# Products of the h and o layers of three batches issued as twins on the two column halves of TensorE

## The chip, the cores and the metric

The kernel runs on one core of a Trainium2 chip. The metric is the time of one execution on the device in microseconds. A profiled execution shows five engines: TensorE (PE, with its weight loads as PEld), VectorE (DVE), ScalarE (ACT), GpSimd (POOL) and SyncE (SP, which issues most DMAs).

## The reference

```python
# attention: 4 batches, 8 heads, 768 positions, 64 wide; proj is 64 x 6
q_bits = (q @ proj > 0); k_bits = (k @ proj > 0)
q_bucket = sum(q_bits * 2**arange(6)); k_bucket = sum(k_bits * 2**arange(6))
scores = where(q_bucket[:, None] == k_bucket[None, :], q @ k.T / 8, -1e9)
x = softmax(scores) @ v                      # heads side by side: (4, 768, 512)
# mixing and channel layer: w_ch1 is 512 x 2048, w_ch2 is 2048 x 512
u = x + real(fft(fft(x, axis=1), axis=2))
un = (u - mean(u)) / sqrt(var(u) + 1e-6)     # over the 512 channels
out = u + maximum(un @ w_ch1, 0) @ w_ch2
```

All inputs and the output are fp32.

## The kernel before

**Attention.** Two heads are handled together; the index n runs over the 16 pairs of heads (4 per batch), and c over six tiles of 128 key positions. For each n and c, `weigh` computes the scores transposed: two products per half of the queries, one per head. Their contraction has 64 rows, so head 0 stands on the upper 64 rows of the array and head 1 on the lower 64 (`sc`, L885). ACT takes the exponential (L889). `values` (L906) multiplies by the values. Each of its products has 64 stationary columns: head 0 stands on the array's left column half and head 1 on its right, and the two share a PSUM bank, on different partitions (`oo`). These are the value products that the title's twins resemble. For one pair, six such steps accumulate.

**Buckets.** `prepare(n+1)` makes the bucket masks for the next pair while the current one runs. `bits` (L817) is four products with 32 columns each and leaves, in the 128 rows of `bt`, the bits of queries and keys of both position halves, 32 rows each. For the pairs 0 to 4 (`LITE`) the bits go straight into the scores as an additional product (L878). For pairs 5 to 15, two more groups follow. `qb` (L831) spreads a number per query over all 128 partitions: for each head h, one product per position half g, with the 32 rows of that half and a table `pw` of powers of two. `kb` (L841) has six tiny products, 128 key positions by two heads each. Then one DVE instruction per head and c compares them and masks the exponentials (L895).

**Mixing.** `mix(b)` does the two Fourier transforms of batch b as products with tables (`cs` L1078, `A` and `B` L1107).

**The channel layer.** `mlp7(b)` computes both layers by a scheme with seven products in place of eight for a 2 by 2 split. The first layer is `h` (`product` at L1371, matmul at L1382): for each of 8 pairs of 128-row blocks there are seven products p1 to p7, each of two steps (k) of 128 by 128 stationary values against 384 moving columns. `h_p` is their PSUM bank. The second layer is `o` (`product` in `outer7`, matmul at L1262): two halves of three tile pairs with seven products of four steps, each 128 by 128 against 256 columns. Each of these results is evacuated from PSUM by ACT or DVE, and combined by DVE. `across` (L1133) transposes rows of x between them.

**Order of the work.** A batch's mixing and channel layer is laid between the attention steps of the next batch: the loop at L1503 takes one step of `attention(b)` and then so many steps of `other`, the generator of `mix(b-1)`, that both end together. So batches 0 to 2 have their h and o products among scores and value products, and batch 3 has them alone, at the end. A scheduler sets each engine's order after that, except in the block under `manual_schedule` (L1473), where the order is as written. `behind()` (L858) puts a product with a raised priority after the last one that was noted in `last[0]`:

```python
with tc.issue_after(last[0].ins), tc.high_priority(offset=AHEAD):
    yield
```

It is used for scores, values, `qb` and `kb`. The h and o products carry no such note. PSUM banks come in three pools of two: `ps_sc` (scores, qb, kb; two banks each), `ps_o` (oo) and `ps_1` (all else, h and o among it), handed out in turn.

Of the kernel before, what the change touches and what calls it, by code (L numbers as in the profile page):

```python
# [11 lines left out]
F32 = mybir.dt.float32  # L12
BF16 = mybir.dt.bfloat16
# [7 lines left out]
P = 128  # L21
B, H, S, D = 4, 8, 768, 64
# [27 lines left out]
def _consts():  # L50


    s = np.arange(HALF)
    freq = np.concatenate([2 * np.arange(NK), 2 * np.arange(NK) + 1])
    ang = 2.0 * np.pi * (np.outer(s, freq) % S) / S
    seq = np.stack([np.cos(ang), np.sin(ang)])
    seq = seq.reshape(2, NT // 2, P, 2 * NK).transpose(2, 0, 1, 3)


    d = np.arange(DM // 2)  # L60
    ang = 2.0 * np.pi * (np.outer(d, np.arange(DM)) % DM) / DM
    sin = -np.sin(ang)
    sin[0] = 1.0 - 2.0 * (np.arange(DM) % 2)
    chan = np.concatenate([np.cos(ang), sin]).reshape(NDC, P, DM).transpose(1, 0, 2)

    off = np.zeros((P, 2))
    for h in range(2):
        off[h * D : h * D + NBITS] = 0.5  # L70
        off[h * D + NBITS] = (NBITS / 4.0, -1.0)


    pw = np.zeros((P, 2, P))
    for r in range(P):
        h, bit = divmod(r % 32, NBITS)
        if h < 2:
            pw[r, h] = 2.0**bit


    d = np.arange(DM // 2)
    fr = np.concatenate([np.arange(DM // 2 + 1), np.arange(1, DM // 2)])
    ang = 2.0 * np.pi * (np.outer(d, fr) % DM) / DM
    ch = np.where(np.arange(DM) <= DM // 2, np.cos(ang), np.sin(ang))
    ch = ch.reshape(2, P, DM // 2, 2).transpose(1, 0, 3, 2)

    s = np.concatenate([np.arange(2, HALF // 2, 2), np.arange(1, HALF // 2, 2)])  # L90
    rows = np.concatenate([s, [0, HALF // 2], s])
    kind = np.repeat([0, 1, 2, 3], [len(s), 1, 1, len(s)])
    sq = np.zeros((2, 2, P, HALF + 1))
    for par in range(2):
        cols = slice(par * NK, HALF + 1 if par else NK)
        ang = 2.0 * np.pi * (np.outer(rows, freq[: HALF + 1][cols]) % S) / S
        for k in range(2):
            own = kind == (0 if par == k else 3)
            own |= (kind == 1) & (k == 0) | (kind == 2) & (k == par)
            w = np.where(own[:, None], np.sin(ang) if k else np.cos(ang), 0.0)  # L100
            w = w.reshape(NT // 2, P, -1)
            sq[0, k, :, cols] = w[0 if par == k else 2]
            sq[1, k, :, cols] = w[1]
    sq = sq.transpose(2, 0, 1, 3)
    return {
        "pw": np.ascontiguousarray(pw, dtype=np.float32),
        "ch": np.ascontiguousarray(ch, dtype=np.float32),
        "sq": np.ascontiguousarray(sq, dtype=np.float32),
        "seq": np.ascontiguousarray(seq, dtype=np.float32),
        "chan": np.ascontiguousarray(chan, dtype=np.float32),  # L110

        "off4": np.ascontiguousarray(np.tile(off[:32], (4, 1)), dtype=np.float32),
        "off": np.ascontiguousarray(off, dtype=np.float32),
    }
# [367 lines left out]
def _main(  # L482
# [109 lines left out]
    nc.gpsimd.memset(pj, 0.0)  # L592
    for h in range(2):
        nc.sync.dma_start(pj[h * D : (h + 1) * D, h * NBITS : (h + 1) * NBITS], proj)
    pw = const.tile([P, 2, P], BF16, tag="pw", name="pw")
    ones = const.tile([P, 32], F32, tag="ones", name="ones")
    nc.gpsimd.memset(ones, 1.0)
    mhalf = const.tile([P, 1], F32, tag="mhalf", name="mhalf")
# [150 lines left out]
    def prepare(n):  # L749
# [76 lines left out]
        for h in range(2):  # L826
            ps = ps_sc.tile([P, 2, 512], F32, tag="sc", name=f"qb{n}_{h}")
            for g in range(2):
                rows = slice(32 * g, 32 * g + 32)
                with behind() if g + h else nullcontext():  # L830
                    last[0] = nc.tensor.matmul(  # L831
                        ps[:, g, 0:HALF], pw[rows, h, :], bt[rows, :],
                        start=True, stop=True,
                    )
            evac(qb[:, h, :].rearrange("p (g s) -> p g s", g=2), ps[:, :, 0:HALF])
        ps = ps_sc.tile([P, 2, 512], F32, tag="sc", name=f"kb{n}")
        for c in range(NT):
            g, i = divmod(c, NT // 2)
            rows = slice(64 + 32 * g, 96 + 32 * g)
            with behind() if c else nullcontext():  # L840
                last[0] = nc.tensor.matmul(  # L841
                    ps[:, g, 2 * i : 2 * i + 2], bt[rows, i * P : (i + 1) * P],
                    pw[rows, :, 0], start=True, stop=True,
                )
        nc.vector.tensor_copy(
            kb.rearrange("p h (g i) -> p g i h", g=2),
            ps[:, :, 0:NT].rearrange("p g (i h) -> p g i h", h=2),
        )
        preps[n] = ts["q"], ts["k"], qb, kb

# [177 lines left out]
    def fold(b, cp):  # L1028
# [6 lines left out]
        for pc in range(2):  # L1035
# [22 lines left out]
            )  # L1058
            yield

    def mix(b):
        x = xs[b]
        yield from fold(b, 1)
        z = zs[b]


        hd = DM // 2
        F = wt([P, 2, 2, 2, DM], F32, "F", f"F{b}", 1)
        nc.gpsimd.memset(F[:, :, 1, :, 0 : hd + 1 : hd], 0.0)
        for par in range(2):  # L1070
            for t in range(NT // 2):
                ps = pt([P, DM], f"cs{b}_{par}_{t}")
                kinds = (0, 1) if t == 1 else (par ^ (t // 2),)
                for pc in range(2):
                    lo = 0 if 0 in kinds else hd // 2 + 1 - pc
                    hi = hd if 1 in kinds else hd // 2 + 1 - pc
                    for cp in range(2):
                        nc.tensor.matmul(  # L1078
                            ps[:, pc + 2 * lo : pc + 2 * hi - 1 : 2],
                            z[:, cp, pc, par, t * P : (t + 1) * P],  # L1080
                            ch[:, cp, pc, lo:hi], start=(cp == 0), stop=(cp == 1),
                        )
# [14 lines left out]
                yield  # L1097

        for j in range(NDC):
            pa, pb = (pt([P, HALF + 1], f"{nm}{b}_{j}") for nm in "AB")
            for par in range(2):
                cols = slice(par * NK, HALF + 1 if par else NK)
                for k, ps in enumerate((pa, pb)):
                    for t in range(2):
                        nc.tensor.matmul(  # L1107
                            ps[:, cols], F[:, par, k, t, j * P : (j + 1) * P],
                            sq[:, t, k, cols], start=(t == 0), stop=(t == 1),
                        )  # L1110

            for ps, op in (pa, ALU.add), (pb, ALU.subtract):
                for i in range(2):
                    u = x[:, j, i * HALF : (i + 1) * HALF].rearrange("p (r n) -> p r n", r=2)
                    if i == 0:
                        f = ps[:, 0 : 2 * NK - 1]
                        f = bass.AP(f.tensor, f.offset, [f.ap[0], [NK, 2], [1, HW]])
                    else:
                        f = ps[:, HW : HALF + 1]
                        f = bass.AP(f.tensor, f.offset, [f.ap[0], [HW, 2], [-1, HW]])  # L1120
                    nc.vector.tensor_tensor(
                        u, u, f, op=op if (j < 2) ^ i else ALU.add
                    )
            yield

        yield from mlp7(b)
# [110 lines left out]
    def outer7(b, half, hall, ut, rs, s1s):  # L1237
# [14 lines left out]
        for j in range(GT):  # L1252
# [4 lines left out]
            def product(a, i, ps=None):  # L1257
# [1 line left out]
                if start:  # L1259
                    ps = pt([P, HD], f"o{b}_{half}_{j}_{i}")  # L1260
                for r in range(HF // 2):
                    nc.tensor.matmul(  # L1262
                        ps, a[:, r], right7[i][:, r], start=start and r == 0,
                        stop=r == HF // 2 - 1, skip_group_check=not start,
                    )
                if j == GT - 1 and (b < B - 1 if half else b > 0):
                    nc.sync.dma_start(right7[i], bd[1 - half, i])
# [57 lines left out]
    def mlp7(b):  # L1325
# [45 lines left out]
        def product(i, ps, start=True):  # L1371
# [7 lines left out]
                    c, r = (0 if i == A11 else 2), (f + HF if i == A22 else f)  # L1379
                    left = w1[:, c : c + 2, r * P : (r + 1) * P]  # L1380
            for k in range(2):
                nc.tensor.matmul(  # L1382
                    ps, left[:, k], right[i][:, k],
                    start=start and k == 0, stop=k == 1, skip_group_check=not start,
                )
            done[0] += 1
            fetch()
# [85 lines left out]
    with tc.manual_schedule(engines={ET.PE, ET.DVE, ET.Activation, ET.Pool}):  # L1473
# [5 lines left out]
                next(other, None)  # L1479
        for _ in other:  # L1480
            pass
        pwf = wt([P, 2, P], F32, "ef", "pwf", 1)
        nc.sync.dma_start(pwf, cn["pw"].ap())
        nc.scalar.copy(pw, pwf)
        means = []
# [100 lines left out]
```

## Time and profile before

| what | value |
|---|---|
| median of 3 runs (lowest to highest) | 1102.68 us (1102.34 to 1106.73) |
| span of the profiled execution | 1100.8 us |
| that execution's own time beside its span | not recorded apart; the fastest run shown is 1.5 us and the median 1.9 us above the span |
| mean granted clock of TensorE | 0.995 |
| PE busy | 1054.5 us, 96% |
| PEld busy | 629.4 us, 57% |
| DVE, ACT, POOL busy | 786.5, 500.6, 58.6 us |
| o products on PE (L1262, three groups) | 259.4 + 42.3 + 3.9 us |
| h products on PE (L1382, five groups) | 163.1 + 105.5 + 23.8 + 23.7 + 12.8 us |
| values on PE (L906), scores on PE (L885) | 155.1, 159.8 us |

Busy time is the union of an engine's records. A row of a group reads: line, engine, operation, what it writes and reads, the shape (rows by columns of the array, then the moving operand), the number of records, then busy time and mean duration, then the engine's idle time before it and what ended that. A timeline row reads: start, length, engine, line, operation, shape and how many records were merged in it.

### The profile page before, as it was taken

Reading aid. Unit: us, or ns where it says so; the run is one execution under the profiler, and the core shown is the slowest. Engines: PE = TensorE matmul, PEld = TensorE weight load, DVE = VectorE, ACT = ScalarE, POOL = GpSimd, SP = SyncE. Lnnn points to the kernel's source line nnn. Section 1 sums busy time; section 2 is a strip of 40 time slices with the busy share of each in tenths; the row PEclk is TensorE's granted clock in tenths of the full one; section 3 lists DMA queues with packets and bytes.
Section 4 is the critical chain, followed back from the end, with each engine's and each line's share of the span. In section 5 each row is a group of like instructions: output and inputs, shape, how many; then the busy total and the mean of one; then the engine's idle time right before and its main releaser. Section 6 shows DMA issues by size and latency. Waiting matters only on the chain.

```text
span 1100.8 us, 14127 instructions
## 1 busy us (share of the span) xinstructions
PE 1054.5 (96%) x4933; PEld 629.4 (57%) x4933; DVE 786.5 (71%) x1321; ACT 500.6 (45%) x1055; POOL 58.6 (5%) x132
## 2 busy tenths in 40 slices
PE   7999997999989999999999999999999999999996
PEld 2333354446744675545664576645674569768675
DVE  5798958868699977776767785965856785644353
ACT  6888555653276324454326433355315522340420
POOL 0000000002000020010000011001000002100000
PEclk9999999999999999999999999999999999999998
DMA  8745443441056161322144134213032205122401
GB/s 224 221 90 119 76 123 88 149 147 26 20 139 210 46 204 34 66 61 70 26 157 108 48 73 162 44 39 96 15 121 75 68 24 172 54 82 85 126 20 41
DMA packets 175566, 103.13 MB, mean 94 GB/s; under 512 B 129408, under 2 KB 162816, under 8 KB 175488
## 3 DMA queue, kind: packets, MB, share of 16 engines
q1 hardware_dynamic: 169696, 88.65, 29.9%
q0 software_dynamic: 4224, 13.11, 3.8%
q8 instruction: 41, 0.67, 0.3%
q10 hardware_dynamic: 1568, 0.39, 0.2%
q14 instruction: 37, 0.30, 0.1%
HBM read 81.14 MB, written 20.97 MB: 93 GB/s over the span
## 4 chain that ended last, share of the span: by engine, by line
PE 63%; DVE 11%; ACT 4%; DMA 2%; issue 2%; DVEq 0%; SPq 0%; ACTq 0%
PE o L1262 22%; PE h_p L1382 21%; PE oo L906 7%; PE sc L885 6%; DVE pk L895 3%; PE cs L1078 2%; PE A L1107 2%; DMA zraw<-in_moe_w_ch_dram 2%; PE B L1107 1%; DVE acc L980 1%; ACT rr L940 1%; PE bits L817 1%; DVE w L1274 1%; DVE h L1248 1%; PE un L1133 1%
## 5 line engine op out<-in xcount | busy, mean ns | idle before, releaser
L1262 PE MATMUL o<-w,h 128*128 128x256 f32 x1152 | 259.4, 382 | 1.2 <-ACT tq L1281 0.7
L1262 PEld LDWEIGHTS o<-w,h 128*128 128x128 f32 x1152 | 216.3, 190 | 43.6 <-issue 4.6
L889 ACT ACTIVATE pk<-sc 128x768 f32<-128x768 f32 x192 | 148.5, 809 | 81.6 <-PE sc L885 64.5
L1382 PE MATMUL h_p<-x,w 128*128 128x384 f32 x448 | 163.1, 494 | 3.2 <-ACT h L1404 1.7
L885 PE MATMUL sc<-qt,kt 64*128 64x384 f32 x768 | 159.8, 519 | 5.4 <-ACT pk L889 5.1
L906 PE MATMUL oo<-pk,vn 128*64 128x385 f32 (+1 forms) x768 | 155.1, 499 | 4.0 <-DVE pk L895 3.3
L895 DVE SCALAR_TENSOR_TENSOR pk<-qb,kb,pk 128x768 f32<-128x768 bf16 x132 | 129.0, 1013 | 29.5 <-ACT pk L889 29.4
L1382 PEld LDWEIGHTS h_p<-x,w 128*128 128x128 f32 x448 | 82.0, 190 | 70.6 <-ACT pk L889 5.4
L980 DVE TENSOR_TENSOR acc<-acc,pk 128x1536 f32<-128x1536 f32 (+1 forms) x72 | 105.8, 1483 | 6.1 <-ACT pk L889 5.4
L1382 PE MATMUL h_p<-w 128*128 128x384 f32 x288 | 105.5, 489 | 2.3 <-ACT w L1419 2.3
L906 PEld LDWEIGHTS oo<-pk,vn 128*64 128x64 f32 x768 | 49.1, 136 | 97.8 <-issue 68.7
L885 PEld LDWEIGHTS sc<-qt,kt 64*128 64x128 f32 x768 | 62.9, 185 | 56.1 <-issue 29.6
L1382 PEld LDWEIGHTS h_p<-w 128*128 128x128 f32 x288 | 53.7, 190 | 41.7 <-ACT w L1419 3.5
L1292 ACT COPY tq<-o 128x256 f32<-128x256 f32 x24 | 8.9, 373 | 105.1 <-PE o L1262 105.1
L1274 DVE SCALAR_TENSOR_TENSOR w<-o,rs,w 128x256 f32<-128x256 f32 x56 | 26.8, 479 | 41.6 <-PE o L1262 41.6
L1262 PE MATMUL o<-w 128*128 128x256 f32 x176 | 42.3, 383 | 1.4 <-DVE w L1274 1.3
L1408 DVE TENSOR_TENSOR h<-h 128x384 f32<-128x384 f32 x32 | 17.8, 556 | 32.2 <-ACT h L1407 32.2
L1281 ACT COPY tq<-o 128x256 f32<-128x256 f32 x24 | 8.9, 371 | 69.3 <-PE o L1262 69.2
L1262 PEld LDWEIGHTS o<-w 128*128 128x128 f32 x176 | 32.8, 190 | 8.8 <-DVE w L1274 3.0
L1016 POOL DMA_DIRECT2D out_dram<-w x30 | 16.4, 548 | 388.8 <-issue 293.2
L1415 DVE TENSOR_TENSOR h<-h 128x384 f32<-128x384 f32 x32 | 17.7, 553 | 26.9 <-ACT h L1414 26.8
L1308 DVE TENSOR_TENSOR tq<-tq,o 128x256 f32<-128x256 f32 x24 | 10.0, 418 | 34.7 <-PE o L1262 34.7
(170 smaller groups left out, 1329.1 us busy)
## 6 DMA issues: line engine op xcount, KB each, us to landing
w<-ad SPq DMA_DIRECT2D x168, 128.0 KB, 2.0
w<-bd SPq DMA_DIRECT2D x42, 512.0 KB, 4.5
zraw<-in_moe_w_ch_dram POOLq DMA_DIRECT2D x16, 512.0 KB, 4.1
bd<-w SPq DMA_DIRECT2D x14, 512.0 KB, 4.2
vn<-in_v_dram SPq DMA_DIRECT2D x32, 192.0 KB, 3.4
qn<-in_q_dram SPq DMA_DIRECT2D x120, 48.0 KB, 2.4
kn<-in_k_dram SPq DMA_DIRECT2D x60, 96.0 KB, 3.4
zraw<-in_moe_w_ch_dram SPq DMA_DIRECT2D x8, 512.0 KB, 5.7
```

What stands on the lines that cost most here:

```text
L885: last[0] = nc.tensor.matmul(ps[:, h, 0:HALF], kt[rows, ks], qt[rows, qs], start=kb is not None, stop=True,)
L889: nc.scalar.activation(pk[:, g, :, 0:HALF], ps[:, :, 0:HALF], AF.Exp, scale=SCALE)
L895: nc.vector.scalar_tensor_tensor(w, qb[:, h].rearrange("p (g s) -> p g s", g=2), kb[:, h, c : c + 1], w, op0=ALU.is_equal, op1=ALU.mult,)
L906: nc.tensor.matmul(oos[g][h * D : (h + 1) * D, 0:w], nat["v", n][:, (2 * c + h) * D : (2 * c + h + 1) * D], pk[:, g, h, 0:w], start=(c == ...
L980: nc.vector.tensor_tensor(acc[:, g], (first if c == 1 else acc)[:, g], new[:, g], op=ALU.add,)
L1078: nc.tensor.matmul(ps[:, pc + 2 * lo : pc + 2 * hi - 1 : 2], z[:, cp, pc, par, t * P : (t + 1) * P], ch[:, cp, pc, lo:hi], start=(cp == 0) ...
L1107: nc.tensor.matmul(ps[:, cols], F[:, par, k, t, j * P : (j + 1) * P], sq[:, t, k, cols], start=(t == 0), stop=(t == 1),)
L1262: nc.tensor.matmul(ps, a[:, r], right7[i][:, r], start=start and r == 0, stop=r == HF // 2 - 1, skip_group_check=not start,)
L1274: nc.vector.scalar_tensor_tensor(t[:, cols], src, r, t[:, cols], op0=ALU.mult, op1=ALU.add)
L1382: nc.tensor.matmul(ps, left[:, k], right[i][:, k], start=start and k == 0, stop=k == 1, skip_group_check=not start,)
L1408: nc.vector.tensor_tensor(c21, c12, c21, op=ALU.add)
L1415: nc.vector.tensor_tensor(c22, c21, c22, op=ALU.add)
```

## The change

It issues every h and o product of batches 0 to 2 as two products with 64 stationary columns each, on the left and the right column half, which together give what the one product gave. Batch 3 keeps full products. The bucket products also take that form: `qb` now enters all 128 rows of `bt`, with a table that is zero outside the 32 rows wanted, twice per head and position half, and `kb` takes 64 key positions at a time, against a table of four columns. The table `pw` has four blocks of 65 columns in place of two of 128.

```diff
-    pw = np.zeros((P, 2, P))
+    pw = np.zeros((P, 4, D + 1))
...
-            pw[r, h] = 2.0**bit
+            at = slice(0, D) if r < D else slice(D, D + 1)
+            pw[r, 2 * (r // 32 % 2) + h, at] = 2.0**bit
...
             for g in range(2):
-                rows = slice(32 * g, 32 * g + 32)
-                with behind() if g + h else nullcontext():
-                    last[0] = nc.tensor.matmul(
-                        ps[:, g, 0:HALF], pw[rows, h, :], bt[rows, :],
-                        start=True, stop=True,
-                    )
+                for i in range(2):
+                    with behind() if i + g + h else nullcontext():
+                        last[0] = nc.tensor.matmul(
+                            ps[i * D : (i + 1) * D, g, 0:HALF], pw[:, 2 * g + h, 0:D], bt,
+                            start=True, stop=True,
+                        )
...
         for c in range(NT):
-            g, i = divmod(c, NT // 2)
-            rows = slice(64 + 32 * g, 96 + 32 * g)
+            i, half = divmod(c, 2)
             with behind() if c else nullcontext():
                 last[0] = nc.tensor.matmul(
-                    ps[:, g, 2 * i : 2 * i + 2], bt[rows, i * P : (i + 1) * P],
-                    pw[rows, :, 0], start=True, stop=True,
+                    ps[half * D : (half + 1) * D, 0, 4 * i : 4 * i + 4],
+                    bt[:, i * P + half * D : i * P + (half + 1) * D],
+                    pw[:, :, D], start=True, stop=True,
                 )
...
+    def multiply(ps, left, right, start, stop, check, halved):
+
+        for i in range(2) if halved else (None,):
+            at = slice(0, P) if i is None else slice(i * D, (i + 1) * D)
+            nc.tensor.matmul(
+                ps[at, :], left[:, at], right, start=start, stop=stop, skip_group_check=check
+            )
...
                 for r in range(HF // 2):
-                    nc.tensor.matmul(
-                        ps, a[:, r], right7[i][:, r], start=start and r == 0,
-                        stop=r == HF // 2 - 1, skip_group_check=not start,
+                    multiply(
+                        ps, a[:, r], right7[i][:, r], start and r == 0,
+                        r == HF // 2 - 1, not start, b < B - 1,
                     )
...
             for k in range(2):
-                nc.tensor.matmul(
-                    ps, left[:, k], right[i][:, k],
-                    start=start and k == 0, stop=k == 1, skip_group_check=not start,
+                multiply(
+                    ps, left[:, k], right[i][:, k], start and k == 0, k == 1,
+                    not start, b < B - 1,
                 )
```

More of the change, by code (lines that the diff above doesn't have):

```diff
@@ L594, in _main @@
         nc.sync.dma_start(pj[h * D : (h + 1) * D, h * NBITS : (h + 1) * NBITS], proj)
-    pw = const.tile([P, 2, P], BF16, tag="pw", name="pw")
+    pw = const.tile([P, 4, D + 1], BF16, tag="pw", name="pw")
     ones = const.tile([P, 32], F32, tag="ones", name="ones")
@@ L837, in prepare @@
         for c in range(NT):
-            g, i = divmod(c, NT // 2)
-            rows = slice(64 + 32 * g, 96 + 32 * g)
+            i, half = divmod(c, 2)
             with behind() if c else nullcontext():
                 last[0] = nc.tensor.matmul(
-                    ps[:, g, 2 * i : 2 * i + 2], bt[rows, i * P : (i + 1) * P],
-                    pw[rows, :, 0], start=True, stop=True,
+                    ps[half * D : (half + 1) * D, 0, 4 * i : 4 * i + 4],
+                    bt[:, i * P + half * D : i * P + (half + 1) * D],
+                    pw[:, :, D], start=True, stop=True,
                 )
         nc.vector.tensor_copy(
-            kb.rearrange("p h (g i) -> p g i h", g=2),
-            ps[:, :, 0:NT].rearrange("p g (i h) -> p g i h", h=2),
+            kb.rearrange("p h (g i) -> p i g h", g=2),
+            ps[:, 0, 0 : 2 * NT].rearrange("p (i g h) -> p i g h", g=2, h=2),
         )
@@ L1481, in _main @@
             pass
-        pwf = wt([P, 2, P], F32, "ef", "pwf", 1)
+        pwf = wt([P, 4, D + 1], F32, "ef", "pwf", 1)
         nc.sync.dma_start(pwf, cn["pw"].ap())
```

## The prediction

> **What bounds the kernel now.** I read the page's busy shares first, then busy time by stage, then TensorE's timeline.
>
> ```profile
> PE 1054.5 (96%) x4933; PEld 629.4 (57%) x4933; DVE 786.5 (71%) x1321; ACT 500.6 (45%) x1055; POOL 58.6 (5%) x132
> ...
> L1262 PE MATMUL o<-w,h 128*128 128x256 f32 x1152 | 259.4, 382 | 1.2 <-ACT tq L1281 0.7
> ...
> L1382 PE MATMUL h_p<-x,w 128*128 128x384 f32 x448 | 163.1, 494 | 3.2 <-ACT h L1404 1.7
> ...
> L906 PE MATMUL oo<-pk,vn 128*64 128x385 f32 (+1 forms) x768 | 155.1, 499 | 4.0 <-DVE pk L895 3.3
> ```
>
> The reader should see that TensorE is busy for 96% of the span, and that o and h products are its largest users. By stage (PE busy time is the second number):
>
> ```profile
> 215.00:400.00 185.00, 174.52 (x769) 105.25 (x768) 155.08 (x288) 87.53 (x191) 14.84 (x27) 0.99 0.37 105
> 400.00:660.00 260.00, 256.13 (x1188) 154.77 (x1188) 191.25 (x292) 109.24 (x232) 14.23 (x31) 1.00 0.32 83
> 660.00:920.00 260.00, 256.77 (x1185) 156.74 (x1184) 188.54 (x293) 102.98 (x217) 15.31 (x33) 1.00 0.25 72
> ```
>
> From 400 to 920 us TensorE idles 7 of 520 us, so time added to or taken from its queue there is time of the kernel. From 215 to 400 it idles 10 of 185 us behind DVE and ACT, and that stage can swallow some of either.
>
> A PE record's end is modelled, so I price by starts. TensorE's timeline gives them (start, then length; names as on the page):
>
> ```profile
> 535.69 1.51 PE L906 MATMUL oo<-pk,vn 128*64 128x385 f32 x8
> 537.14 3.72 PE L1262 MATMUL o<-w,h 128*128 128x256 f32 x16
> 540.79 1.56 PE L885 MATMUL sc<-qt,kt 64*128 64x384 f32 x8
> 542.28 1.51 PE L906 MATMUL oo<-pk,vn 128*64 128x385 f32 x8
> 543.72 1.99 PE L1262 MATMUL o<-w 128*128 128x256 f32 x8
> ...
> 619.62 1.45 PE L1382 MATMUL h_p<-x,w 128*128 128x384 f32 x4
> 620.91 1.45 PE L1382 MATMUL h_p<-w 128*128 128x384 f32 x4
> 622.30 1.56 PE L885 MATMUL sc<-qt,kt 64*128 64x384 f32 x8
> ```
>
> Each fp32 product of the program is two records. From 619.62 to 620.91 are 4 records of h: 0.3225 us each in steady flow; o takes 0.216 (single starts). A value visit of 8 records takes 542.28 to 543.72, 1.44 us. Its twins start 7 ns apart, so it is 4 slots; starts within it are 0.374, 0.324, 0.325 and, to the next engine shape, 0.419 apart. So a twin slot costs 0.324 (0.325 where both steps have 384 columns) and the visit pays **0.05 at its start and 0.095 at its end**. The o visit takes 537.14 to 540.79, 3.65 us for 16 records: 3.46 steady plus **0.10 at the start and 0.09 at the end**. The scores visit pays the same 0.10 and 0.09. A transpose visit starts for 0.055, the 32-column forms for 0.025, the 32-row bucket form for almost nothing; all end for 0.09.
>
> **What the Trainium skill says.** "TensorEngine Tiling (Array Packing)", Key Properties: changing the tiling mode, not just the tile, drains TensorE, while different tiles run in parallel. The trace agrees: 0.09 us at every change of shape, and none between halves. "TensorE: Matmul & The Clock Gate", LDWEIGHTS: a load's time follows its columns, not its rows. The trace agrees in direction (64 columns 136 ns, 128 columns 190 ns), and it fits the 0.05 against 0.10 at the start. The same page, The mechanism: matmuls start in strict program order. In the trace, at 194 to 205 us single value halves with h products between them ran alone, each for a whole slot pair. Perfetto Trace Analysis, Tensor Engine Instruction: the end of a PE record is computed, not observed; hence starts only.
>
> **The change, step by step.** I compared the order in which the instructions stand on TensorE in both programs, and priced it with the numbers above.
>
> *Shapes.* Value and h or o products now share one shape, and so do the bucket products. Changes of shape fall from 453 to 397: 56 x 0.094 = **-5.3 us**. Of the starts, 41 of h and 27 of o at 0.104 become 19 and 8 at 0.051 (-5.7); seven value starts vanish (-0.4), while four more transpose starts, two more of scores and a few others come (+0.7): **-5.3 us**.
>
> *Twins in place of full products.* Batches 0 to 2 have 336 products of h and 504 of o, 1680 slots. A twin slot of 384 columns takes 0.323 to 0.325 against 0.3225; I take 1 ns more: **+1.7 us** (0 to 4.2). A twin with 256 moving columns isn't in the trace. The nearest row is o itself: two 64-column loads of 136 ns, 7 ns apart, end within its 0.216 slot, so the same 1 ns stands.
>
> *Lone halves.* The scheduler now places each half by itself. In some 30 places it puts something between two halves: bucket columns, scores, transposes, or another product. What follows in the queue then pairs out of step until the shape changes, and a half is left alone at an end. Walking both orders with starts in program order and each half busy for two slots, one half works alone for 7.8 us before (value halves only) and 23.9 after (h 15.2, o 3.5, values 5.2). A lone half wastes half of its time: (23.9-7.8)/2 = **+8.0 us**. Scores of n=9 and n=13 are also split by value products: two more pair times of 0.645, **+1.3 us**.
>
> *Buckets*, 11 preparations (n=5 to 15). Before, qb is two slots of four 32-row matmuls, 0.166 each by starts; now all 128 rows enter, so it is four slots with one half of the columns each: 11 x 0.33 = **+3.6 us**. A bf16 twin isn't in the trace; its stream length is that of the row shown, and its 64 weights are fewer than the 128 loaded in 0.091 now, so I keep 0.166. The six kb matmuls take 0.07 in all now; three pairs that load 64 columns each may take 0.07 to 0.2: **+0.7 us** (0 to 1.5). The evacuations and the small DVE copy move as many elements as before: 0.
>
> Sum on TensorE: -5.3 - 5.3 + 1.7 + 8.0 + 1.3 + 3.6 + 0.7 = **+4.7 us**. By stage that is about -1.4 with batch 0's products (up to about 400 us), +3.3 with batch 1's, +2.6 with batch 2's, and +0.2 after.
>
> *Waits.* From 400 to 920 us the trace lists all of these:
>
> ```profile
> PE h_p L1382 <- ACT w L1419: 2.3, 2, 1.1
> PE kb L841 <- ACT qb L533: 1.8, 2, 0.9
> PE o L1262 <- DVE w L1274: 1.3, 3, 0.6
> PE h_p L1382 <- ACT h L1414: 0.9, 1, 0.9
> ```
>
> The kb waits are at n=9 and n=13, where kb stands right behind qb and needs qb's bank evacuated. In the new order A and B products stand between them, so these waits are filled: **-1.8 us**. If they stayed, the sum would be 1.8 higher. The other waits follow from evacuations that don't change. DVE, ACT, SP and POOL get the same number of instructions; only their order moves, mostly below 300 us. The ad and bd loads are issued by SP as often as before, each after its product, and land in 2 to 4.5 us ahead of 12 buffers of use; they queue on nothing new: 0. If that cover went, one late ring load would cost up to its 2 us.
>
> So +2.9 us on the profiled execution. Its span is 1100.8 us, and the runs shown have the median 1102.68, 1.9 us more for what lies around it. I take that over: 1102.68 + 2.9 = **1105.5 us**.
>
> **The rivals.**
>
> *A, faster: lone halves and splits cost nothing.* The 9.3 us of lone halves and split scores could stand where TensorE waits anyway. Then -10.6 + 1.7 + 4.3 - 1.8 = -6.4, 1096.3 us. For it speaks batch 0, where a dozen of the splits stand and PE idles 10 of 185 us. Against it, most of them are after 400 us, where only 7 us of idle time exists.
>
> *B, slower: a bank comes free late.* 54 of 186 twin products run out of step. A bank is asked for again two products later: 2 x 1.29 us less the product's own 1.29 and ACT's copy of 0.48 leave about 0.8 us of slack. A step of 0.65 fits in. A half that stands 1.9 to 2.4 us behind its partner (six products of batches 1 and 2) does not, and TensorE would wait 1.1 to 1.6 us each in place of the waits filled: +6.6 to 9.6 above my sum, 1112 to 1115 us. It decides from a lag over 0.8 us. Against it, other work stands behind most of these halves and gives ACT the time.
>
> *C, slower: TensorE can't be fed.* An o twin slot needs two loads and two matmuls in 0.217 us, 54 ns per record, for long stretches. The densest 8 us of the trace hold 124 records, 65 ns each. If that were the limit, 1008 slots would grow by 0.04: +45 us, 1150 us. Against it, 1 us of the trace holds 36 records, and the TensorE page gives about 81 ns for a load and a matmul together (Back-to-back issue gap), which as an estimate is 162 ns for four records.
>
> *D: the halves don't run together at all.* Then 672 x 0.3225 + 1008 x 0.216 = +434 us. The value twins, 7 ns apart, speak against it.
>
> **How the numbers follow.** My forecast 53%, A 13%, B 27%, C 5%, D 2%. The forecast's own ends are about 1100 (twins free, kb at 0, batch 0 hides its lone halves) and 1110 (twins at 2.5 ns, waits not filled, batch 0's saving lost in waits for DVE). About 0.5%, 5.5 us, is what a measurement of this kernel can tell from no change: below 1097.2 or above 1108.2. The forecast falls within that for 42 points, slower for 10, faster for 1; A gives 9 faster and 4 the same; B 22 slower and 5 the same; C and D are slower. So: faster 0.10, same 0.51, slower 0.39. Range 1098 to 1114: it leaves out part of A, the end of B, and C and D.
>
> **What would show it.** Right: no gap of 0.09 between value and h or o records; the first h twin 0.05 late, not 0.10; twin slots of o near 0.217; h and o halves without a partner, some 30 of them; qb in four slots; kb waits at n=9 and n=13 gone. Wrong: o slots at 0.25 or more (C), PE waits for ACT h or w above 10 us from 400 to 920 us (B), PE time there no longer than before (A).

## The result and the profile after

| | before | after |
|---|---|---|
| median of 18 runs each, us (lowest to highest) | 1102.51 (1100.6 to 1106.73) | 1107.47 (1105.71 to 1110.93) |
| span of the profiled execution, us | 1100.8 | 1105.6 |

The ratio is 1.0043, with the interval 1.0033 to 1.0052: the change costs 3.6 to 5.7 us. I had forecast 2.9 us more, 1105.5, within 1098 to 1114. The sign came out as forecast and the time lies within the range; of the size, about 2 us are missing. The working behind it did not come out: the cost of halves out of step was put some 5 us too high, and the waits and the stage of batch 0 some 4 us too low each. That the sum comes near the measured time is luck.

The page after shows the same engine rows and, in place of the lines of o, h and values, these (o and h now share L1066, inside `multiply`; each of their products is four records in place of two):

```profile
PE 1055.6 (95%) x6657; PEld 574.4 (52%) x6657; DVE 787.5 (71%) x1321; ACT 500.0 (45%) x1055; POOL 59.0 (5%) x132
...
L1066 PE MATMUL o<-w,h 128*64 128x256 f32 (+1 forms) x2016 | 260.4, 380 | 1.3 <-ACT tq L1290 1.0
...
L1066 PE MATMUL h_p<-x,w 128*64 128x384 f32 (+1 forms) x768 | 169.7, 493 | 5.5 <-ACT h L1413 3.3
...
L907 PE MATMUL oo<-pk,vn 128*64 128x385 f32 (+1 forms) x768 | 153.1, 498 | 3.7 <-DVE pk L896 3.2
```

The reader should see that PE's busy time is the same within 1.1 us, although it has 1724 records more, and that the idle time before h rose from 3.2 to 5.5 us, with the same evacuation as its end (L1413 is L1404 of the kernel before). Busy time by stage (the span's window, its length, then PE, PEld, DVE, ACT and POOL busy time, the granted clock, DMA share and rate):

```profile
215.00:400.00 185.00, 172.37 (x1211) 88.36 (x1207) 151.56 (x276) 85.61 (x187) 13.33 (x25) 0.98 0.36 104
400.00:660.00 260.00, 255.27 (x1760) 135.33 (x1758) 190.43 (x290) 108.37 (x230) 14.18 (x29) 1.00 0.31 82
660.00:920.00 260.00, 255.92 (x1765) 135.27 (x1763) 188.60 (x296) 103.50 (x219) 14.18 (x29) 1.00 0.24 70
```

PE is idle for 12.6 of 185 us in batch 0's stage (10.5 before) and for 8.8 of 520 us behind it (7.1 before). Busy time can't tell where the time went, since it doesn't say how far the queue has come. So I read how far it has come: the start of the first scores of each pair n in TensorE's records. Times are us from the span's start, one profiled execution for each kernel; e1 to e12 are the experiments told below. A dash stands where further work follows the main part. These are single executions: those of e3, e5, e6 and e9 are the fastest of their runs, and that of e8 is 2.5 us above its median. So the table tells where time goes, and the medians tell how much it is in all.

| kernel | n=6 | n=7 | n=8 | n=12 | n=15 | end |
|---|---|---|---|---|---|---|
| before | 243.4 | 315.1 | 409.6 | 669.0 | 841.9 | 1100.8 |
| after | 240.0 | 313.3 | 412.3 | 672.7 | 847.3 | 1105.6 |
| e1 halves kept together | 241.4 | 314.4 | 411.9 | 670.5 | 843.3 | 1101.6 |
| e2 buckets only | 244.2 | 315.9 | 412.8 | 673.0 | 846.8 | 1105.4 |
| e3 twins only | 240.1 | 313.4 | 412.2 | 672.9 | 847.7 | 1105.8 |
| e4 = e1, batch 3 too | 240.7 | 313.5 | 410.6 | 669.2 | 842.0 | 1101.6 |
| e5 before, no test | 239.9 | 312.6 | 407.6 | 666.9 | 839.8 | 1098.5 |
| e6 after, no test | 239.1 | 313.6 | 412.5 | 672.9 | 847.5 | 1105.5 |
| e7 = e1, no test | 238.4 | 313.8 | 413.5 | 672.1 | 845.3 | 1103.4 |
| e8 = e1, batches 1 and 2 only, old buckets | 243.5 | 315.2 | 410.5 | 669.1 | 841.9 | 1100.0 |
| e9 before, no w_ch2 transfers | 239.4 | 311.5 | 405.9 | 665.2 | 838.2 | – |
| e10 after, no w_ch2 transfers | 237.5 | 310.6 | 405.4 | 665.9 | 840.5 | – |
| e11 = e1, no w_ch2 transfers | 234.5 | 307.7 | 402.5 | 661.1 | 834.0 | – |
| e12 = e6, no w_ch2 transfers | 236.1 | 309.3 | 403.6 | 664.3 | 839.2 | 1097.5 |

After minus before is -3.4 us at n=6, -1.8 at n=7, **+2.7 at n=8**, +3.7 at n=12 and +4.8 at the end. So the stage up to the start of n=8, with batch 0's products, loses 2.7 us, batch 1's products lose 1.0 and batch 2's, with what follows, 1.1.

**The steps that held.** TensorE's timeline around one visit (start, length, engine, line, operation, shape, records merged):

```profile
537.71 1.56 PE L886 MATMUL sc<-qt,kt 64*128 64x384 f32 x8
539.20 1.51 PE L907 MATMUL oo<-pk,vn 128*64 128x385 f32 x8
540.54 1.90 PE L1066 MATMUL o<-w,h 128*64 128x256 f32 x16
542.26 1.90 PE L1066 MATMUL o<-w 128*64 128x256 f32 x16
544.09 1.56 PE L886 MATMUL sc<-qt,kt 64*128 64x384 f32 x8
```

The value visit starts at 539.20 and the o products at 540.54, 1.34 us later. Before, the same visit took 1.44: the 0.095 us of its end are gone. The first o group takes 1.72 us for 16 records, eight twin slots of 0.215. The second takes 1.83, which is 1.72 and the 0.1 that a change of shape costs. A twin slot of h, by starts, is 0.3225 us, and the first after another shape is 0.05 longer. All of this is as forecast, except that by these starts a twin slot is no longer than a full one: I had added 1 ns a slot, +1.7 us.

**The waits.** TensorE's waits from 400 to 920 us (in all, times, longest):

```profile
PE o L1066 <- DVE w L1283: 2.3, 3, 1.0
PE h_p L1066 <- ACT w L1428: 2.3, 2, 1.1
PE A L1116 <- DVE x L1130: 1.6, 2, 0.8
PE h_p L1066 <- ACT h L1423: 0.9, 1, 0.9
PE sc L886 <- ACT pk L890: 0.7, 2, 0.3
PE h_p L1066 <- ACT w L1143: 0.5, 2, 0.2
PE o L1066 <- ACT tq L1290: 0.2, 1, 0.2
```

The two kb waits of 0.9 us are gone, as forecast. But the A products that now stand in their place wait themselves for DVE, twice 0.8 us. In all 8.5 us are listed, where 6.3 were before.

### The profile page after: what moved, and what is told of

The parts are those of the page before. It is cut to its first block, busy times and chain, and to the rows that moved or that the text cites. A ratio compares the mean times of both kernels' runs of the same rounds, so it can differ in the third digit from the quotient of the medians.

```text
span 1105.6 us, 17591 instructions
## 1 busy us (share of the span) xinstructions
PE 1055.6 (95%) x6657; PEld 574.4 (52%) x6657; DVE 787.5 (71%) x1321; ACT 500.0 (45%) x1055; POOL 59.0 (5%) x132
## 4 chain that ended last, share of the span: by engine, by line
PE 62%; DVE 11%; ACT 4%; DMA 3%; issue 2%; SPq 0%; DVEq 0%; ACTq 0%
PE o L1066 22%; PE h_p L1066 22%; PE oo L907 6%; PE sc L886 6%; DVE pk L896 2%; PE cs L1087 2%; DVE acc L981 2%; PE A L1116 1%; DMA zraw<-in_moe_w_ch_dram 1%; PE B L1116 1%; ACT rr L941 1%; ACT pk L890 1%; PE un L1142 1%; DVE w L1283 1%; PE bits L818 1%
## 5 line engine op out<-in xcount | busy, mean ns | idle before, releaser
L1066 PE MATMUL o<-w,h 128*64 128x256 f32 (+1 forms) x2016 | 260.4, 380 | 1.3 <-ACT tq L1290 1.0
L1066 PEld LDWEIGHTS o<-w,h 128*64 128x64 f32 (+1 forms) x2016 | 180.4, 144 | 78.2 <-issue 5.6
L1066 PE MATMUL h_p<-x,w 128*64 128x384 f32 (+1 forms) x768 | 169.7, 493 | 5.5 <-ACT h L1413 3.3
L1066 PEld LDWEIGHTS h_p<-x,w 128*64 128x64 f32 (+1 forms) x768 | 74.0, 146 | 78.9 <-issue 43.8
L1066 PE MATMUL h_p<-w 128*64 128x384 f32 (+1 forms) x480 | 109.2, 487 | 2.3 <-ACT w L1428 2.3
L1066 PEld LDWEIGHTS h_p<-w 128*64 128x64 f32 (+1 forms) x480 | 48.3, 147 | 47.3 <-issue 24.6
L1066 PE MATMUL o<-w 128*64 128x256 f32 (+1 forms) x304 | 42.1, 381 | 3.5 <-DVE w L1283 3.4
L1066 PEld LDWEIGHTS o<-w 128*64 128x64 f32 (+1 forms) x304 | 27.4, 145 | 15.3 <-DVE w L1283 5.7
```

The costliest lines, as they stand in the source:

```text
L1066: nc.tensor.matmul(ps[at, :], left[:, at], right, start=start, stop=stop, skip_group_check=check)
```

## The experiments

The questions were: do the halves that go out of step cost the 8.0 us of the prediction; what do the buckets cost; and why does batch 0's stage lose time? Each ratio below is to the kernel before, measured beside it.

**e1: the right half tied behind its left.** `multiply` notes its first product and raises the second behind it:

```diff
+            with ExitStack() as held:
+                if first is not None:
+                    held.enter_context(tc.issue_after(first.ins))
+                    held.enter_context(tc.high_priority(offset=AHEAD))
+                first = nc.tensor.matmul(
```

> The changed kernel, with the right half of every h and o twin tied behind its left half and raised in priority, so that nothing comes between the two halves. Walking its order, one half works alone for 6.5 us in place of 23.9, the scores of n=9 and n=13 are no longer split, and there are 391 changes of shape in place of 397. Theory (TensorE's queue adds up: changes of shape save, lone halves cost): -8.7 for lone halves, -1.3 for scores, -1 for shapes against the changed kernel, so 1096 to 1098 us, some 0.5% faster than the kernel before. Rival 1 (the loss is in waits for ACT and DVE with batch 0's products, which the new order causes, and lone halves fall into waits): at most 3 us less than the changed kernel, 1104 to 1107.5. Rival 2 (changes of shape are worth little): no faster than the kernel before, 1102 or more.

Measured: 1103.38 us, ratio 1.0012 (1.0003 to 1.0022); about 3.4 us of the change's cost go away, where the theory had 11. In the table, e1 takes 258.6 us from n=8 to n=12 and 172.8 from n=12 to n=15, where the change takes 260.4 and 174.6: **1.8 us less in each**. Walking the two orders as the prediction did, starts in program order and a lone half busy for two slots, puts 4.6 and 4.1 us there, split scores and three changes of shape each included. So keeping the halves together gives back less than half of what I charged.

The 1.8 us are a net figure. In each of these two stages e1 has one visit of value products that takes 2.84 us (475.74 to 478.58 in the first), as the kernel before has (473.17 to 476.01), where the changed kernel takes 2.02 (480.91 to 482.93). The second head's products wait there for their mask from VectorE, while the other half works, so TensorE's list of waits doesn't show it. Without these visits e1 would gain some 2.6 us in each stage, an estimate from these starts.

The change's own records show part of why the charge was too high. These are starts of records (us), read from the trace of the kernel after; all are h halves of 384 columns. A record doesn't say on which half it ran; that is read from the distances:

```
499.380 499.386   a pair
499.753 499.760   a pair
500.076           one half alone
500.312           the other half, a new product
500.398           the first half's next
500.686 500.721 501.008 501.043 501.331 501.366   one half each in turn
```

One half comes free at about 500.08, 0.322 us after its start at 499.760, and starts a new product at 500.312, 0.23 us later. In the program's order that product's other half stands ahead of it, and that other half's place is taken until 500.721. So it started out of turn; by the walk it would have stood still until 500.72, for 0.64 us. From 500.686 on the halves are 0.035 us apart, and each repeats every 0.322 us: the offset itself costs nothing more. The Trainium skill, "TensorE: Matmul & The Clock Gate", The mechanism (Part 3), says that matmuls start in strict order, and I took from it that a half would hold the queue up for a full pair. Here the trace differs, and the measurement decides.

If I count only what is left over at changes of shape (the longer half of each run of one shape), the walk gives 1.8 us in each stage between the change and e1. That equals what was measured, but it doesn't show the count to be right: only 0.6 of it are lone halves, the rest split scores (0.6) and changes of shape (0.5), and a run with a half out of step takes longer than it says. The run of 54 records from 569.65 takes 7.81 us, the same run in e1, with the halves together, 7.38. The count has them equal, the walk has 0.65 between them. The cost of a lone half lies between the two.

**e2: only the buckets changed,** h and o full as before:

```diff
-                r == HF // 2 - 1, not start, b < B - 1,
+                r == HF // 2 - 1, not start, False,
```

(and the same in `mlp7`'s `product`).

> Only the bucket products are changed; all h and o products stay full. Shape changes 449 in place of 453. Theory: four qb slots in place of two for 11 pairs, +3.6, kb +0.7, starts of the 64-column shape in place of the 32-row one +0.7, ends -0.4: +4.6 on the kernel before, 1106 to 1108 us. Rival (the spreading stands beside waits for the score banks and costs nothing): within 1 us of the kernel before, 1102 to 1103.5.

Measured: 1106.24 us, ratio 1.0042 (1.0027 to 1.0057), about 4.6 us, as expected in sum. But two thirds of it stand at n=8 (+3.2), behind only four of its eleven preparations (n=5 to 8). The seven behind n=8 cost 1.4 us, where seven elevenths of the sum are 2.9, so the price of one preparation isn't confirmed. And batch 0's stage loses time here too, without any twin of h or o.

**e3: only the twins,** with `qb`, `kb` and `pw` as before:

> The twins of h and o stay, the bucket products are those of the kernel before. Lone halves as in the changed kernel (24.2 us), 428 changes of shape in place of 397. Theory: buckets -4.3 against the changed kernel, 31 more changes of shape +2.9 at their ends and +0.6 at starts: about -0.8, 1106 to 1107.5 us. Rival (shape changes around the buckets cost nothing, the wide bucket products are a plain loss): -4.3, 1103 us.

Measured: 1108.82 us, ratio 1.0069 (1.0056 to 1.0083), more than either the theory or the rival had. With its twins alone the change is no better than as a whole, so the two costs don't add up. The theory's reason is that the old buckets stand among the twins and bring changes of shape back, 31 of them against the change as a whole. That fits in direction; why e3 is slower still, by 1.3 us or more, isn't shown.

**e4: e1 with batch 3 as twins too** (`b < B - 1` becomes `True`). Batch 3's products stand alone, so this adds 560 twin slots and hardly any change of shape.

> As e1_pairs_kept, with batch 3 as twins too: 112 products of h and 168 of o more, 560 slots, in a stage without attention. Theory: a twin slot costs what a full one costs to within 1 ns, so 0 to +0.6 us on e1_pairs_kept, and o slots of 0.216 to 0.217 in that stage. Rival (feeding TensorE four records in 0.216 us fails in long stretches): o slots of 0.25 or more for 336 slots, at least +11 us on e1_pairs_kept.

Measured: 1104.12 us, ratio 1.0014 (1.0003 to 1.0026), 0.7 us over e1's median with overlapping intervals; both spans are 1101.6. A twin slot costs about 1 ns more than a full one, or nothing; the runs don't tell these apart. Rivals C (feeding) and D (one half after the other) fall, at 45 and 434 us.

**e5, e6, e7: is ScalarE too busy in batch 0's stage?** In that stage ScalarE converts w_ch2's slices beside the evacuations of h. Two of its instructions per slice test the range of the words. They were left out for w_ch2 in the kernel before (e5), the changed one (e6) and e1 (e7):

```diff
-        nc.scalar.activation(t, hi, AF.Abs)
-        nc.scalar.activation(
-            t, t, AF.Relu, bias=least, scale=-1.0, accum_out=strange[:, col : col + 1]
-        )
+        if col < NDC * DFF // WC:
+            ... the same, for w_ch1 alone
```

> The kernel before, without the two ACT instructions (with their accumulator read) per slice of w_ch2 that look for weights outside the range of the quick conversion; the slices are converted as before. 16 slices of about 1.6 us of ACT work go, all of it in the stage of batch 0's products. Theory (that stage is paced by ACT's queue, which is why time saved on TensorE there is lost): 3 to 8 us less than the kernel before, 1094 to 1099 us. Rival (DVE or the arrival of weights paces it): within 2 us of the kernel before.

> The changed kernel with the same ACT instructions left out (the check of w_ch2's range). Theory: with ACT out of the way the saving on TensorE in batch 0's stage (about 5 us of fewer changes of shape, halves running freely) is kept: 0 to 4 us less than e5_before_no_act_check, in place of 5 us more. Rival (the saving is lost elsewhere than behind ACT): again about 5 us more than e5_before_no_act_check.

> e1_pairs_kept with the same ACT instructions left out. Theory: batches 1 and 2 give 1.8 us each as from the changed kernel to e1_pairs_kept, so 3 to 5 us less than e6_after_no_act_check and 3 to 8 less than e5_before_no_act_check. Rival: no faster than e5_before_no_act_check.

Measured: 1103.41 (ratio 1.0011, 1.0003 to 1.0019), 1109.91 (1.0075, 1.0059 to 1.009) and 1105.09 (1.0021, 1.0008 to 1.0034). Nothing got faster, and before and after stand no closer than they did. Less work on ScalarE doesn't help by itself. But with its instructions out of the way, e6's timeline shows what they had covered (a bracket gives the idle time of the engine and what ended it):

```profile
330.55 0.68 ACT L642 ACTIVATE zraw<-zraw 128x512 int32<-128x512 uint32 x1 [3.97 <-DMA zraw<-in_moe_w_ch_dram]
330.72 0.69 DVE L638 SCALAR_TENSOR_TENSOR w<-zraw,w 128x512 int32<-128x512 int32 x1
331.13 0.47 ACT L1421 ACTIVATE h<-h_p 128x384 f32<-128x384 f32 x1
331.50 0.47 ACT L1424 COPY h<-h_p 128x384 f32<-128x384 f32 x1
331.65 0.20 PEld L1067 LDWEIGHTS h_p<-x,tq 128*64 128x64 f32 x4 [3.26 <-ACT h L1421]
331.65 2.16 PE L1067 MATMUL h_p<-x,tq 128*64 128x384 f32 x12 [2.60 <-ACT h L1421]
```

ScalarE waited 3.97 us for a slice of w_ch2 to land. Behind that conversion, in ScalarE's order, stood the evacuation of h that TensorE needed, and TensorE waited 2.60 us in its turn. The list of waits names the evacuation, but the wait began with a transfer. From 200 to 410 us, ScalarE's waits for these slices in e6 are

```profile
ACT zraw L642 <- DMA zraw<-in_moe_w_ch_dram: 17.6, 8, 4.0
```

The kernel before has 4.8 us in the same row, the changed one 6.2.

**e8: twins only where they pay.** This is e1 with batch 0 as full products too (`0 < b < B - 1`) and the old buckets. If batch 0's stage is what spoils the change, this should leave that stage alone and keep batches 1 and 2. It differs from e1 in two things at once, though, and doesn't separate them.

> Twins only for batches 1 and 2, the two halves kept together, with full products for batch 0 and batch 3 and the bucket products of the kernel before. Theory: batch 0's stage is as in the kernel before; batches 1 and 2 save about 2.0 us each in changes of shape, less about 0.4 us each in waits: 1098.5 to 1100.5 us, some 0.3% faster than the kernel before. Rival (twins bring nothing on the chip even where halves stay together): 1102 us or more.

Measured: 1099.33 us, **ratio 0.9972 (0.9959 to 0.9986)**: faster than both kernels. In the table its n=6 and n=7 are those of before, and n=8 is within a microsecond. From n=8 on it gains: 258.6 and 258.1 us for the stages n=8 to 12 and n=15 to the end, where before takes 259.4 and 258.9. From n=8 to 15 it takes the times of e1 (258.6 and 172.8 us), so behind n=8 the new buckets cost e1 nothing that shows. Its stages 400 to 660 and 660 to 920:

```profile
400.00:660.00 260.00, 255.13 (x1712) 131.72 (x1712) 191.56 (x293) 109.79 (x233) 15.03 (x32) 1.00 0.32 83
660.00:920.00 260.00, 255.87 (x1769) 131.26 (x1767) 188.81 (x294) 103.24 (x218) 16.39 (x34) 1.00 0.25 74
```

PE busy time is 1.0 and 0.9 us below that of before.

**e9, e10, e11: without w_ch2's transfers.** Only the first two slices are fetched; later conversions work on what lies in the two raw buffers, so o is multiplied by other weights. Each engine keeps its number of instructions in the main part. But the scheduler also orders some 30 to 40 of ScalarE's instructions anew in e9 and e10, about half of them conversions.

```diff
-            self.fetch(i + self.depth)
+            if self.col == 0:
+                self.fetch(i + self.depth)
```

> The kernel before, with only the first two slices of w_ch2 fetched: the later slices' conversions run on the words that the two raw buffers already hold, so the o products of all batches use wrong weights; the work of every engine stays, only the transfers of the later w_ch2 slices are gone. It is the yardstick of the next two. Theory (the stage of batch 0 up to about 410 us is paced by the arrival of w_ch2's slices, because evacuations of h stand behind conversions in ScalarE's order): a little faster than the kernel before, 1097 to 1101, ratio 0.995 to 0.999, the start of batch 2's first scores 0 to 4 us earlier. Rival (the arrival of the slices paces nothing): within 1 us of the kernel before.

> The changed kernel with the same transfers left out (o products with wrong weights). Theory: without the transfers batch 0's stage keeps what its saved changes of shape are worth (about -5 by the trace's prices, of which some goes to halves that wait), batches 1 and 2 still cost +1.1 each, so its median stands -4 to +1 us against the same kernel before without the transfers, 1095 to 1100. Rival (something else in batch 0's order keeps the products waiting, such as evacuations that come late whatever the weights do): again +3 to +6 us, 1101 to 1106.

> The changed kernel with the right half of every twin tied behind its left, and the same transfers left out (o products with wrong weights). Theory: 3 to 5 us less than the changed kernel without the transfers, so 4 to 8 us below the kernel before without them (ratio 0.993 to 0.996), because the halves no longer wait for one another in any batch. Rival: 3 to 5 us less than the changed kernel without the transfers too, but within 1.5 us of the kernel before without them.

The medians, 3084.67, 3105.84 and 3098.81 us, say nothing on this. The words left in the raw buffers trip the range test, so the kernel's general branch for unusual inputs (`_any_scores`) ran behind the main part and took 2 ms. I had not foreseen that. The main part runs ahead of it, so the table's starts up to n=15 can be read. At n=8 the kernel before gains 3.7 us, the changed one 6.9 and e1 9.4. **After minus before is then -0.5 us at n=8 in place of +2.7**, and e1 minus before is -3.4 in place of +2.3. From n=8 to n=15 the distances are the old ones within a microsecond: after loses 2.8 more here and 2.7 with the transfers; e1 gains 0.8 here and 0.9 there. So leaving the transfers out moves the stage of batch 0 and, within a microsecond, nothing behind it, and it helps most the kernel that is then furthest ahead. At n=15 the changed kernel is still 2.3 us behind, where the theory had 1 at most. This rests on one trace of each. It also doesn't separate the slices' landing from ScalarE's new order: at 326 us of the changed kernel a conversion stands ahead of the evacuation of h (326.02, 326.57), and at the same place of e10 behind it (323.80, 323.44).

**e12: e6 without the transfers,** to have a median too.

> The changed kernel without the range test of w_ch2's slices (two ScalarE activations and their reading per slice), and with only the first two slices of w_ch2 fetched (o products with wrong weights). The test has to go too, because it finds odd words in the reused buffers and sends the program into its general branch, which adds 2 ms. Compared with the changed kernel without the test alone (1109.9). Theory (the arrival of the slices paces batch 0's stage, and what is gained there lasts to the end): 1101 to 1105, so 5 to 9 us less, as the traces of the pair with the transfers and without them have it at 840 us (847.3 and 840.5). Rival (the gain at 410 us is given back behind it): 1107 to 1111.

Measured: 1098.53 us (1097.62 to 1103.07), ratio 0.9977 (0.9967 to 0.9986), 11.4 us less than e6. The theory's direction held; its 5 to 9 us were too small. The kernel before without test and transfers was not run, so this shows what the two together cost the changed kernel, and not that they cost the kernel before less. At n=8 it is 8.9 us ahead of e6, and the spans differ by 8.0. Part of the rest is in the clock: averaged over the timed runs, the granted clock was 0.997 here and 0.993 in e6, which is up to 4 us of 1100. Among ScalarE's waits from 200 to 410 us no row is left in which `zraw` waits for a DMA; one of 4.4 us in which it waits for VectorE is. The gain at n=8 is not given back later, so the rival falls.

## Why the prediction was right, and where its working was not

**Right for its number, by luck: its errors cancel.** Forecast +2.9, measured +4.8 in the profiled executions. By stage, with the forecast's waits of -1.8 shared between batches 1 and 2:

| stage | forecast | measured |
|---|---|---|
| batch 0's products (to n=8) | -1.4 | +2.7 |
| batch 1's (n=8 to 12) | +3.3 - 0.9 | +1.0 |
| batch 2's and after (n=12 to the end) | +2.6 - 0.9 + 0.2 | +1.1 |

- **Shapes, -5.3 and -5.3:** right in their prices. The end of a visit costs 0.095, a twin starts for 0.05, and between values and o there is nothing. e3, without the new buckets, is no faster, which fits a saving that takes twins and buckets together.
- **Twins, +1.7:** not confirmed. By starts, twin slots in the change last as long as full ones; 560 more of them in e4 cost 0.7 us, which the runs don't tell from nothing.
- **Lone halves, +8.0 and split scores, +1.3:** the first step that failed, by its size. It assumed that a half out of step holds the queue for a whole pair time, 0.64 us. In the records a half starts its next product out of turn, 0.23 us after it comes free, and runs on. Measured with e1, tying the halves gives 1.8 us in each of batches 1 and 2 (3.6; some 5.2 without the two value visits), where the same walk has 8.7. The direction (halves apart cost time, and tying them together gives some of it back) was right. The walk also took the value visits from the order alone. The one in each stage that waits for a mask went from 2.84 to 2.02 us, a gain of some 1.6 us in all that the sum lacks.
- **Buckets, +3.6 and +0.7:** near as a sum, by e2's 4.6. But two thirds of e2's loss stand at n=8, behind four of eleven preparations; how the cost divides between the buckets' own slots and batch 0's stage isn't settled.
- **Waits, -1.8:** failed in part. The kb waits went, but A took their place and waits for DVE; the waits listed rose by 2.2 us in place of falling. The forecast named what fills the gap and didn't ask whether the filler was ready.
- **Batch 0's stage, -1.4:** the second step that failed. I priced it on TensorE alone, having written myself that 215 to 400 us is a stage that idles behind others. There the changed kernel gets ahead (-3.4 us at n=6) and then waits, for h evacuations that come late in ScalarE's order:

```profile
PE h_p L1066 <- ACT h L1413: 3.1, 1, 3.1
PE h_p L1066 <- ACT h L1420: 1.3, 1, 1.3
```

These are its longest waits from 310 to 410 us; the longest of before there are

```profile
PE h_p L1382 <- ACT h L1404: 1.5, 1, 1.5
PE h_p L1382 <- ACT w L1419: 1.0, 1, 1.0
```

The longest is the same evacuation in both, L1413 now and L1404 before. ScalarE was not idle ahead of it:

```profile
324.60 0.76 ACT L650 ACTIVATE zraw<-zraw,least 128x512 f32<-128x512 f32 x1
325.24 0.20 ACT L650 ACTIVATION_READ_ACCUMULATOR zraw<-zraw,least 128x1 f32 x1
325.33 0.80 ACT L890 ACTIVATE pk<-sc 128x768 f32<-128x768 f32 x1
326.02 0.66 ACT L642 ACTIVATE zraw<-zraw 128x512 int32<-128x512 uint32 x1
326.57 0.48 ACT L1413 COPY h<-h_p 128x384 f32<-128x384 f32 x1
327.10 2.83 PE L1066 MATMUL h_p<-x,w 128*64 128x384 f32 x8 [3.09 <-ACT h L1413]
```

It did the rest of a range test, an exponential and a conversion first, and waited for no transfer among them. So here the wait comes from the order of ScalarE's work, and in e6 from a transfer. This wait lasts 2.9 to 3.1 us in e1 to e4 as well, e2 without a twin of h or o among them, 1.5 in e8, and 2.4 in e10, without the transfers. Why the order puts the evacuation late in all these kernels isn't shown.

I had put the ad and bd loads at zero and not named the w_ch2 transfers. Leaving them out, with the new order that comes with it, takes away 3.2 us of the miss of 4.1 in the traces (+2.7 with them, -0.5 without). How much of this is the clock isn't settled: the changed kernel works for 6.0 us at half clock behind this wait, some 3.0 us lost by estimate, and the kernel before for 3.4 us at 227, some 1.7; e10 has 3.4 us of it at 172 and e9 none. The rest is open.

**Rivals.** A (lone halves free) falls: the kernel is not faster, and tying the halves gives 3.6 us back in batches 1 and 2. B (a bank comes free late) has a likeness, a late evacuation, but in batch 0 and behind other work of ScalarE rather than behind halves out of step; the 10 us of h waits from 400 to 920 that would have shown it are 3.7. C and D are refuted by the slots of 0.215. The 81 ns that I set against C are in the Trainium skill, "TensorE: Matmul & The Clock Gate", Back-to-back issue gap, the figure for 128 moving columns; an o slot has 256, so my estimate of 162 ns went beyond what it states, and the measured slot decides.

## What to carry to other kernels

Before pricing a change on the engine that is busy, find the stages that something else paces: there a saving can turn into a wait. e8 keeps the twins out of such a stage, ties the halves and has the old buckets, and is a gain (ratio 0.9972, where the whole change gave 1.0043); how much each of the three brings isn't separated. When products are split into halves, keep the halves together in the queue: that gave 3.4 us back here. Where the profile names an evacuation as what ended a wait, look at what stands ahead of it in that engine's order. It may be other work, as in the changed kernel, or a transfer, as in e6. And when an experiment takes something away, see whether the scheduler has also changed the order.

## What the hardware showed that I had not expected

**Column halves run on out of step within a shape.** The starts above show it: 0.322 us per half, the two 0.007 or 0.035 us apart, with no loss from the offset itself. What costs is the place where they part: there one half stood still for 0.23 us before it started its next product, ahead of its turn.

**Behind some idle stretches TensorE runs at half clock for a while.** The changed kernel waited 3.1 us, from 324.0 to 327.1 us; the granted clock (third number from the end) was

```profile
316.00:326.00 10.00, 8.01 (x50) 2.96 (x48) 9.37 (x20) 8.98 (x24) 0.80 (x2) 1.00 0.79 199
326.00:333.00 7.00, 5.90 (x20) 2.27 (x22) 4.68 (x5) 2.95 (x8) 0.26 (x1) 0.52 0.38 117
333.00:343.00 10.00, 10.00 (x62) 4.27 (x60) 8.69 (x22) 8.01 (x19) 0.53 (x1) 1.00 0.47 125
```

The Trainium skill, "TensorE: Matmul & The Clock Gate", What's actually happening, has half rate after an idle window of about 3.4 us. The trace agrees in the lengths: half clock lasts from 326.3 to 333.1, two such windows, and in the kernel before for one of 3.4 us at 227. It differs in what goes before. Half clock began 2.3 us into the wait here, and at 227 behind a wait of 2.0 us. It doesn't follow every wait either: e1 and e4 have the same wait of 3.1 us and stay at full clock behind it (e1: 1.00 from 328.6 to 335.6), and in e5 there is none before the last 10 us. So a wait of 3 us in this kernel can cost some 3 us more behind it, or nothing, and single traces differ by that much.
